# Fourteen of the 64 pieces of w2 split among the experts instead of in the blocks before them, with ScalarE issuing their transfers

## The chip, the core and the metric

The kernel runs on one core of a Trainium2 chip. The metric is the device time of one execution in microseconds (us); lower is better. The profile counts the granted TensorE clock as a share of 2.4 GHz: 1.00 is 2.4 GHz, 0.50 is 1.2 GHz.

## The reference

Three layers follow each other, all in float32 at the outside.

1. Attention without a softmax: for each of 8 batches and 8 heads, `kv = k^T v`, `out = q kv`, and each row of `out` is divided by its root mean square and multiplied by `g_norm`. This gives `x` with 4608 rows (8 x 576 tokens) and 512 columns.
2. A dense layer: `h = x w_in` (2048 columns), `g = h cos(h)`, `x = g w_out` (512 columns).
3. A mixture of 8 experts: for each token the gate `x w_gate` chooses one expert; the expert computes `relu(x w1[e]) w2[e]` (512 to 1024 to 512 columns), and the row is multiplied by the gate's probability.

## The kernel before

Every float32 matrix product is made of float16 products: an operand is split into a high and a low half, and three matmuls (high by high, high by low, low by high) are summed in PSUM. A split is one ScalarE instruction (high half) and, behind it, one VectorE instruction (low half); the helper `split` holds both, at lines 103 and 104.

The work runs in two parts.

**Blocks 0 to 8.** Each block takes 512 of the 4608 tokens through the dense layer, in 32 steps; the code calls a step `hs`, and step h of block b has the number 32 b + h in the lists below. In each step TensorE makes a part of the dense layer's two products for this block, while the other engines prepare the attention of the next block, split its k and v (tiles ks), and route the block before to the experts. The order of everything is written out by hand: lists say in which step a helper is called. From block 4 on the dense layer's first product is made with seven products for eight (tiles sx and sy, results h); it reads sums of weights that `w_fac` (block 2 and 3) and `w_fac4` (block 3 and 4, the fourth sum, four groups g of three steps i) make on VectorE. Block 3 lies at about 315 to 403 us, block 4 up to 487, block 5 up to 572, block 6 up to 656, block 7 up to 745, block 8 up to 827.

**Experts 0 to 7.** For each expert the tokens' rows come from DRAM (`load_x`), then come the first product (`e_g1` for expert 0, `e_g1q` for the others, again seven products for eight, tiles qx and qy), relu, the second product (`e_g2`, and `e_g2t` for the last 96 rows), and the scatter to the result. Meanwhile the weight sums and row sums of the next expert are made (`prepare`, with the lists `prep0`, `prep` and `side`: "f" is a split of a weight sum, "s" a sum, "x" and "y" the row sums). `e_g1q` calls `side` four times, twice for each of two groups.

**w2.** The second weights of all experts are 64 pieces of 128 x 512 float32 (piece i belongs to expert i // 8). Each is loaded by `w2_load` (256 KB), split by `w2_split` into a high and a low half, and stored by `w2_store` to the DRAM array `w2x` (256 KB); `load_w2x(e)` later brings all halves of an expert back. `W2_AT` lists the step of each piece's split; all 64 stand in blocks 2 to 8. The first 51 use the pools w2p (loads, two buffers) and w2q (halves, tile w2o, two buffers), and the load of piece i + 2 is issued behind the split of piece i. The 13 of block 8 use free places of xring in the same manner. A store is issued two steps after its split, in block 8 one step after. All these transfers are issued on SP, in the order of the program, with all other loads, stores and transposes.

At the start of block 7 SP also loads all kv matrices at once (`load_kv_all`, tile kvall, eight transfers of 256 KB). In the blocks 4 and 5 the pieces of k and v are split in the steps of `KV_AT` (five pairs: k, v) and multiplied in those of `KV_MM` (tile kvps).

Of the kernel before, what the change touches and what calls it, by code (L numbers as in the profile page):

```python
# [9 lines left out]
F32 = mybir.dt.float32  # L10
# [26 lines left out]
def tile_attn_moe_moe(ctx: ExitStack, tc: tile.TileContext, q, k, v, g_norm, w_in, w_out, w_gate, w1, w2, out):  # L37
    nc = tc.nc
    B, H, S, D = q.shape
    NT, DM = out.shape  # L40
# [3 lines left out]
    E, _, F2 = w1.shape  # L44
    KD = DM // 128
    NFB = DFF // 128
    NF2 = F2 // 128
# [6 lines left out]
    FAST = 4  # L54
# [17 lines left out]
    w2x = dram.tile([E, 128, 2, 4096], F16, name="w2x")  # L72
# [39 lines left out]
    def now(f):  # L112
        if f is not None:
            f()
# [36 lines left out]
    xring = ctx.enter_context(tc.tile_pool(name="xring", bufs=1)).tile([128, 11 * 1024], F16, name="xring")  # L151
# [8 lines left out]
    pools = {}  # L160
# [812 lines left out]
    w2st, w2o = {}, {}  # L973

    def w2_place(n):

        n = (x_slot(NB - 1, "11") + 7 + n) % 11
        return xring[:, n * 1024:n * 1024 + 1024]

    def w2_load(i):  # L980

        e, fb = divmod(i, NF2)
        if i < W2_LAST:
            w2st[i] = pools["w2p"].tile([128, DM], F32, tag="w2i", name="w2i")
        else:
            w2st[i] = w2_place(i % 2).bitcast(F32)
        nc.sync.dma_start(out=w2st[i], in_=w2[e, fb * 128:(fb + 1) * 128, :])

    def w2_split(i):
        if i < W2_LAST:  # L990
            w2o[i] = pools["w2q"].tile([128, 2, DM], F16, tag="w2o", name="w2o")
        else:
            w2o[i] = w2_place(2 + i % 2).rearrange("p (a c) -> p a c", a=2)
        lo = split(w2o[i][:, 0], w2o[i][:, 1], w2st.pop(i), S_W2)

        def late():
            lo()
            if i + 2 < W2_LAST or W2_LAST <= i < E * NF2 - 2:
                w2_load(i + 2)

        return late

    def w2_store(i):
        e, fb = divmod(i, NF2)
        nc.sync.dma_start(out=w2x[e, :, :, fb * DM:(fb + 1) * DM], in_=w2o.pop(i))

    def load_w2x(e):
        if e < 2:
# [10 lines left out]
    def load_x(e, r0=0, r1=CAP):  # L1019
        if r0 == 0:  # L1020
            xeT[e] = xtp.tile([128, 2 * KD, CAP], F16, name="xeT")
            fld[e] = xsm.tile([128, CT, FLD], F32, name="fld")
        rows = slice(e * NT + r0, e * NT + r1)
        nc.sync.dma_start_transpose(out=xeT[e][:, :, r0:r1], in_=xs.bitcast(F16)[rows, 0:2 * DM])
        i0, i1 = r0 // 128, (r1 + 127) // 128
        nc.sync.dma_start(out=fld[e][:, i0:i1],
                          in_=xs[e * NT + i0 * 128:e * NT + i1 * 128, DM:ROW].rearrange("(i p) c -> p i c", p=128))
# [39 lines left out]
    HC = CAP // 2  # L1067
# [63 lines left out]
    def e_g1q(e, side):  # L1131

        h1[e] = (h1p.tile([128, NF2, CAP], F16, name="h1h"), h1p.tile([128, NF2, CAP], F16, name="h1l"))
        hh, hl = h1[e]

        def out(p, r, src):
            nc.scalar.activation(out=hh[:, p, r], in_=src, func=AF.Relu)
            return lambda: nc.vector.scalar_tensor_tensor(out=hl[:, p, r], in0=src, scalar=0.0, in1=hh[:, p, r],
                                                          op0=ALU.max, op1=ALU.subtract)

        r0, r1, both = slice(0, HC), slice(HC, CAP), slice(0, CAP)
        for g in range(2):
            st = []
            for n in range(2):
                p = 2 * g + n
                x, y = [(psm if n else psh).tile([128, HC], F32, tag="m" if n else "h", name=nm) for nm in ("qx", "qy")]
                e_prod(e, 1, p, x, first=True)
                t5, t1 = [b3.tile([128, HC], F32, tag=tag, name="qt") for tag in "nu"]
                nc.scalar.activation(out=t1, in_=x, func=AF.Copy)
                st.append((p, x, y, t1, t5, wq["hc"][n]))  # L1150
            for p, x, y, t1, t5, hc in st:
                e_prod(e, 2, p, y, first=True)
                nc.vector.tensor_tensor(out=hc[:, 1], in0=y, in1=t1, op=ALU.add)
            side()
            tvs = []
            for p, x, y, t1, t5, hc in st:
                e_prod(e, 6, p, x)
                tvs.append(b2.tile([128, HC], F32, tag="yT", name="qt"))
                nc.scalar.activation(out=tvs[-1], in_=x, func=AF.Copy)
                e_prod(e, 5, p, y, first=True)  # L1160
                nc.scalar.activation(out=t5, in_=y, func=AF.Copy)
            side()
            late = []
            for (p, x, y, t1, t5, hc), tv in zip(st, tvs):
                e_prod(e, 7, p, x)
                e_prod(e, 3, p, y)
                c22 = b3.tile([128, HC], F32, tag="u", name="c22")
                nc.vector.tensor_tensor(out=c22, in0=x, in1=t5, op=ALU.add)
                nc.vector.tensor_tensor(out=hc[:, 0], in0=y, in1=tv, op=ALU.add)
                now(out(p + 4, r0, c22))  # L1170
                late.append(out(p, both, hc[:, 0:2].rearrange("p r c -> p (r c)")))
            late[0]()
            for p, x, y, t1, t5, hc in st:
                e_prod(e, 4, p, x)
                now(out(p + 4, r1, x))
            late[1]()
# [85 lines left out]
    for e in range(E):  # L1262
        for c in range(2):
# [20 lines left out]
    FAC_AT = {h: divmod(i, 6) for i, h in enumerate(  # L1284
        [64 + h for h in (0, 1, 2, 4, 6, 8, 10, 12, 14, 16, 18, 24, 26, 28, 30)] + [
            96 + h for h in (0, 1, 2, 6, 8, 10, 12, 14, 16)])}
    FAC4_AT = [(g, i, 32 * (FAST - 1) + h) for g, hs in enumerate(((20, 21, 21), (24, 25, 25), (32, 41, 42), (43, 47, 48)))
               for i, h in enumerate(hs)]
    W2_AT = [64 + 7 * i // 3 for i in range(14)] + [98 + 7 * i // 2 for i in range(9)] + [32 * n + h for n, hs in (
        (4, (30, 31)), (5, (2, 9, 11, 15, 31)), (6, (2, 9, 10, 15, 17, 19, 25, 27, 30, 31)),  # L1290
        (7, (2, 3, 9, 10, 15, 17, 19, 25, 27, 30, 31)), (8, (3, 6, 9, 10, 13, 15, 17, 19, 22, 23, 25, 27, 30))) for h in hs]
    W2_LAST = sum(h < 256 for h in W2_AT)
    KV_AT = ((16, 17), (17, 18), (19, 19), (26, 27), (27, 30))
    KV_MM = (19, 21, 22, 30)

    with tc.manual_schedule():
        pump()
# [35 lines left out]
        for b in range(NB):  # L1333
# [83 lines left out]
            if b == 1:  # L1417
                todo = [("g", 1, AHEAD), ("y", 0, NFB - 2), ("y", 0, NFB - 1), ("g", 1, AHEAD + 1)]
                ys = [("y", 1, f) for f in range(NFB - LAG)]

                for f in range(AHEAD + 2, NFB):
                    n = 2 if f < AHEAD + LAG + 2 else f - LAG - 2 - ys[0][2] + 1
# [97 lines left out]
            if b >= FAST:  # L1520
# [16 lines left out]
                for hs in range(32):  # L1537
                    g, step = divmod(hs, 8)
# [48 lines left out]
                f()  # L1587
        fac.close()
        p2r = ExitStack()
        h1p = p2r.enter_context(tc.tile_pool(name="h1p", bufs=1, side="right", reuse_waits="tile"))  # L1590
        obp = p2r.enter_context(tc.tile_pool(name="obp", bufs=4, side="right", reuse_waits="tile"))
        wq["hc"] = [xring[:, o:o + 4 * HC].bitcast(F32).rearrange("p (r c) -> p r c", r=2)
# [10 lines left out]
        ranks = [call(r_rank, b)] + [call(r_scatter, b, t) for t in range(4)] + [  # L1603
            call(load_x, e, HEAD, CAP) for e in range(2)] + [call(gates_x, 0, 0, HEAD // 128)]
        hold.append(1)
        prep0 = {4: ("f0",), 5: ("s2",), 6: ("f1",), NF2 + 3: ("x1", "y1", "f6", "f3")}
        prep = (("f1", "x0", "s3", "f4"), ("y0", "x1"), ("f5", "y1", "f2"), ("f6", "f3"), ())
        side = (("s0", "f0"), ("s1",), ("s2",), ())
        later = {}

        def prepare(e, items):
            for it in items:
                if it == "gates":
                    later.pop(it)()
                    continue
                n = int(it[1:])
                if it[0] == "x":
                    later[e, n] = x_sums(e, n)
                elif it[0] == "y":
                    later.pop((e, n))()  # L1620
                else:
                    {"s": w_sums, "f": w_split}[it[0]](e, n)
# [24 lines left out]
        turn, put = e_g2t(0)  # L1647
        turn()
        load_x(2)
        for e in range(1, E):  # L1650
            todo = list(side) if e + 1 < E else []
            if e == 1:
                todo = [(), ("s0",), ("f0", "gates"), ("s1", "s2")]
                later["gates"] = call(gates_x, 1)
                put0 = put
            e_g1q(e, lambda: todo and prepare(e + 1, todo.pop(0)))
            if e + 1 < E:
                load_w2x(e + 1)
            if 2 < e + 2 < E and e + 2 > 2 and e + 2 not in xeT:
                load_x(e + 2)  # L1660
            for n, i in enumerate((0, None, 1, 2, 3)):
                if e + 1 < E:
                    prepare(e + 1, prep[n])
                if i is None:
                    turn, put = e_g2t(e)
                    turn()
                else:
                    e_g2(e, i)
                if n == (3 if e + 1 < E else 2):
                    put()  # L1670
                if e == 1 and n == 3:
                    put0()
            if e + 1 < E:
                gates_x(e + 1)
# [83 lines left out]
```

## Time and profile before

| | |
|---|---|
| three runs | 1222.55, 1223.27, 1223.70 us (median 1223.27) |
| the profiled execution | 1221.86 us, of which the span from the first to the last instruction is 1220.0 |
| busy in the span: TensorE, VectorE, ScalarE, POOL | 1177.7, 906.2, 694.4, 359.0 us |
| mean granted TensorE clock | 0.991 |
| moved by DMA | 188.37 MB, a mean of 154 GB/s |

An engine's busy time is the time in which one of its instructions ran. The end of a matmul is modelled, so rows of matmuls overlap: what separates them is the distance of their starts. Times in the views are counted from the start of the span. A row ends with the idle time of the engine just before it and what ended that idle time, in square brackets or behind the last bar. PE is TensorE, DVE is VectorE, ACT is ScalarE, SP is SyncE; SPq and ACTq are instructions of their queues, such as the issue of a DMA.

### The profile page before, as it was taken

What the parts mean: (1) busy time and instruction counts of PE and PEld (TensorE: products, weight loads), DVE (VectorE), ACT (ScalarE), POOL (GpSimd) and SP (SyncE); (2) the same over time, 40 slices, a digit from 0 to 9 for tenths busy, and PEclk for the clock granted to TensorE, in tenths of its full rate; (3) what the DMA queues carried; (4) which work ended last, traced back from release to release, by engine and by line L of the source; (5) the groups of instructions that cost most, each with busy time, mean ns of one, the idle gap of its engine ahead of it and who ended that gap; (6) DMA issues with size and microseconds to landing.
All of it is one profiled execution on the core that took longest, in us unless ns stands there. A gap on an engine that the chain in (4) does not pass through costs nothing.

```text
span 1220.0 us, 22013 instructions
## 1 busy us (share of the span) xinstructions
PE 1177.7 (97%) x8612; PEld 718.4 (59%) x8612; DVE 906.2 (74%) x1468; ACT 694.4 (57%) x1220; POOL 359.0 (29%) x367
## 2 busy tenths in 40 slices
PE   6989999999999999999998999999999999999996
PEld 6534445444444676666665666665776576576663
DVE  4789955888969798888776676684687777777740
ACT  3665663666666766766755756663455455455441
POOL 1123423334434344244253243251102102102111
PEclk8999999999999999999999999999999999999998
DMA  9669816776754745756538548548396365363001
GB/s 292 209 184 314 263 25 150 203 147 160 196 122 115 181 92 110 178 113 149 130 90 237 167 96 226 139 131 226 85 283 213 78 192 188 71 202 117 27 24 52
DMA packets 278882, 188.37 MB, mean 154 GB/s; under 512 B 209646, under 2 KB 244462, under 8 KB 278768
## 3 DMA queue, kind: packets, MB, share of 16 engines
q1 hardware_dynamic: 272128, 167.68, 53.0%
q0 software_dynamic: 5952, 19.18, 4.4%
q8 instruction: 69, 1.13, 0.4%
q14 instruction: 45, 0.37, 0.1%
q10 hardware_dynamic: 688, 0.02, 0.0%
HBM read 97.86 MB, written 49.38 MB: 121 GB/s over the span
## 4 chain that ended last, share of the span: by engine, by line
PE 76%; DVE 8%; issue 6%; ACT 4%; DMA 3%; POOL 2%; SPq 0%; POOLq 0%; ACTq 0%; DVEq 0%
PE yps L817 12%; PE ops L117 4%; PE ops L119 4%; PE ops L118 4%; PE hps L118 4%; PE hps L119 4%; PE hps L117 4%; PE yps L117 4%; PE yps L119 4%; PE yps L118 4%; PE sx L117 2%; PE sx L118 2%; PE sx L119 2%; PE qx L119 2%; PE qx L117 2%
## 5 line engine op out<-in xcount | busy, mean ns | idle before, releaser
L783 POOL TENSOR_TENSOR gl<-n,gh 128x512 f16<-128x512 f32 x80 | 96.1, 1202 | 248.5 <-ACT gh L782 199.7
L764 POOL TENSOR_TENSOR gl<-u,gh 128x512 f16<-128x512 f32 x64 | 90.2, 1409 | 225.7 <-ACT gh L763 177.8
L1194 POOL DMA_INDIRECT out_dram<-ob,ei x40 | 48.4, 1211 | 302.5 <-ACT ob L1192 281.8
L817 PE MATMUL yps<-woh,gh 128*128 128x512 f16 x328 | 124.8, 380 | 0.5 <-DVE yrow L104 0.4
L817 PE MATMUL yps<-woh,gl 128*128 128x512 f16 x328 | 124.7, 380 | 0.3 <-POOL gl L783 0.3
L817 PE MATMUL yps<-wol,gh 128*128 128x512 f16 x328 | 124.8, 380 | 0.0
L817 PEld LDWEIGHTS <-gh 128*128 128x128 f16 x656 | 63.6, 98 | 64.6 <-issue 2.4
L117 PE MATMUL hps<-xring,wih 128*128 128x512 f16 x256 | 97.0, 379 | 3.3 <-DVE u L766 3.3
L118 PE MATMUL hps<-xring,wih 128*128 128x512 f16 x256 | 97.0, 379 | 1.0 <-ACT xring L577 0.9
L119 PE MATMUL ops<-w2h,h1l 128*128 128x512 f16 x256 | 97.0, 379 | 0.0
L118 PE MATMUL ops<-w2l,h1h 128*128 128x512 f16 x256 | 97.0, 379 | 0.0
L117 PE MATMUL ops<-w2h,h1h 128*128 128x512 f16 x256 | 97.0, 379 | 0.0
L119 PE MATMUL hps<-xring,wil 128*128 128x512 f16 x256 | 97.0, 379 | 0.0
L117 PE MATMUL yps<-woh,gh 128*128 128x512 f16 x248 | 94.0, 379 | 0.2 <-DVE yrow L104 0.2
L119 PE MATMUL yps<-woh,gl 128*128 128x512 f16 x248 | 94.0, 379 | 0.0
L118 PE MATMUL yps<-wol,gh 128*128 128x512 f16 x248 | 94.0, 379 | 0.0
L118 PEld LDWEIGHTS <-wih 128*128 128x128 f16 x576 | 56.5, 98 | 46.9 <-issue 13.0
L778 DVE SCALAR_TENSOR_TENSOR n<-h,n 128x512 f32<-128x512 f32 x60 | 63.9, 1065 | 20.3 <-ACT n L777 18.0
L117 PEld LDWEIGHTS <-wih 128*128 128x128 f16 x576 | 56.5, 98 | 35.5 <-issue 0.7
L119 PEld LDWEIGHTS <-wil 128*128 128x128 f16 x576 | 56.5, 98 | 35.4 <-DVE wst L286 1.2
L782 ACT ACTIVATE gh<-n 128x512 f16<-128x512 f32 x80 | 50.5, 631 | 32.4 <-DVE n L780 32.4
L779 ACT ACTIVATE n<-n,half_pi 128x512 f32<-128x512 f32 x80 | 57.6, 720 | 17.3 <-DVE n L778 17.3
(281 smaller groups left out, 3325.5 us busy)
## 6 DMA issues: line engine op xcount, KB each, us to landing
w1s<-in_moe_w_dram SPq DMA_DIRECT2D x16, 1024.0 KB
w2i<-in_moe_w_dram SPq DMA_DIRECT2D x51, 256.0 KB
w2x<-w2o SPq DMA_DIRECT2D x51, 256.0 KB
xs<-pre SPq DMA_DIRECT2D x8, 1320.0 KB
wst<-in_moe_w_in_dram SPq DMA_DIRECT2D x8, 1024.0 KB
wst<-in_moe_w_out_dram SPq DMA_DIRECT2D x8, 1024.0 KB
w2h<-w2x SPq DMA_DIRECT2D x16, 512.0 KB
w2l<-w2x SPq DMA_DIRECT2D x16, 512.0 KB
```

Of the source, the lines that this page charges most:

```text
L117: nc.tensor.matmul(out=o, lhsT=ah, rhs=bh, start=first, stop=False, **kw)
L118: nc.tensor.matmul(out=o, lhsT=ah, rhs=bl, start=False, stop=False, **kw)
L119: nc.tensor.matmul(out=o, lhsT=al, rhs=bh, start=False, stop=last, **kw)
L764: nc.gpsimd.tensor_tensor(out=gl, in0=u, in1=gh, op=ALU.subtract)
L778: lambda: nc.vector.scalar_tensor_tensor(out=u, in0=h, scalar=sc, in1=n, op0=ALU.mult, op1=ALU.subtract),
L779: lambda: nc.scalar.activation(out=u, in_=u, func=AF.Sin, scale=SIN_SCALE, bias=half_pi),
L782: lambda: nc.scalar.activation(out=gh, in_=u, func=AF.Copy),
L783: lambda: nc.gpsimd.tensor_tensor(out=gl, in0=u, in1=gh, op=ALU.subtract))
L817: nc.tensor.matmul(out=yps[b][t], lhsT=g[k][:, o:o + 128], rhs=w[fb // 8][:, (fb % 8) * 512:(fb % 8) * 512 + 512], start=first and i == 0, ...
L1194: d = nc.gpsimd.indirect_dma_start(out=out, out_offset=bass.IndirectOffsetOnAxis(ap=eid[e, i][r], axis=0), in_=ob[r], in_offset=None, boun ...
```

## The change

- Pieces 50 to 63 of w2 leave `W2_AT`; the other 50 stand there with new steps: 14 in block 2 as before, then 8, 1, 4, 7, 7 and 9 in blocks 3 to 8 (before: 9, 2, 5, 10, 11 and 13).
- The fourteen are loaded into one place of xring, split into a tile w2o of a pool of one buffer (w2r), and stored. Their loads and stores are issued on ScalarE's queue. A new function `piece(e, n)` is called in nine turns n of each expert e from 1 on: it stores the piece that was split before, issues the next load, and in turns 2, 5 and 8 (5 and 8 in expert 1) splits a piece. Turns 0 to 3 are the four calls of `side` in `e_g1q`, turns 4 to 8 stand before the five parts of the second product.
- Groups 0 and 1 of the fourth weight sum move from steps 20, 21, 21 and 24, 25, 25 of block 3 to 17, 18, 20 and 21, 22, 24.
- The third v piece of blocks 4 and 5 is split in step 21 instead of 19, and its matmuls are called in step 23 instead of 22.
- In expert 0 the weight split f1 for expert 1 is made before the second tile of the second product instead of behind the seventh tile of the first.

```diff
         else:
-            w2st[i] = w2_place(i % 2).bitcast(F32)
-        nc.sync.dma_start(out=w2st[i], in_=w2[e, fb * 128:(fb + 1) * 128, :])
+            w2st[i] = (w2_place(i % 2) if i < len(W2_AT) else xring[:, 32 * HC:32 * HC + 1024]).bitcast(F32)
+        queue = nc.sync if i < len(W2_AT) else nc.scalar
+        queue.dma_start(out=w2st[i], in_=w2[e, fb * 128:(fb + 1) * 128, :])
 
     def w2_split(i):
-        if i < W2_LAST:
+        if i < W2_LAST or i >= len(W2_AT):
             w2o[i] = pools["w2q"].tile([128, 2, DM], F16, tag="w2o", name="w2o")
...
-            if i + 2 < W2_LAST or W2_LAST <= i < E * NF2 - 2:
+            if i + 2 < W2_LAST or W2_LAST <= i < len(W2_AT) - 2:
                 w2_load(i + 2)
...
     def w2_store(i):
         e, fb = divmod(i, NF2)
-        nc.sync.dma_start(out=w2x[e, :, :, fb * DM:(fb + 1) * DM], in_=w2o.pop(i))
+        queue = nc.sync if i < len(W2_AT) else nc.scalar
+        queue.dma_start(out=w2x[e, :, :, fb * DM:(fb + 1) * DM], in_=w2o.pop(i))
...
-    FAC4_AT = [(g, i, 32 * (FAST - 1) + h) for g, hs in enumerate(((20, 21, 21), (24, 25, 25), (32, 41, 42), (43, 47, 48)))
+    FAC4_AT = [(g, i, 32 * (FAST - 1) + h) for g, hs in enumerate(((17, 18, 20), (21, 22, 24), (32, 41, 42), (43, 47, 48)))
                for i, h in enumerate(hs)]
-    W2_AT = [64 + 7 * i // 3 for i in range(14)] + [98 + 7 * i // 2 for i in range(9)] + [32 * n + h for n, hs in (
-        (4, (30, 31)), (5, (2, 9, 11, 15, 31)), (6, (2, 9, 10, 15, 17, 19, 25, 27, 30, 31)),
-        (7, (2, 3, 9, 10, 15, 17, 19, 25, 27, 30, 31)), (8, (3, 6, 9, 10, 13, 15, 17, 19, 22, 23, 25, 27, 30))) for h in hs]
+    W2_AT = [64 + 7 * i // 3 for i in range(14)] + [32 * n + h for n, hs in (
+        (3, (4, 7, 9, 11, 13, 15, 29, 31)), (4, (30,)), (5, (9, 11, 15, 31)), (6, (9, 11, 15, 17, 25, 27, 30)),
+        (7, (9, 11, 15, 17, 25, 27, 30)), (8, (3, 6, 9, 11, 13, 17, 22, 23, 27))) for h in hs]
...
-    KV_AT = ((16, 17), (17, 18), (19, 19), (26, 27), (27, 30))
-    KV_MM = (19, 21, 22, 30)
+    KV_AT = ((16, 17), (17, 18), (19, 21), (26, 27), (27, 30))
+    KV_MM = (19, 21, 23, 30)
...
         p2r = ExitStack()
+        pools["w2q"] = p2r.enter_context(tc.tile_pool(name="w2r", bufs=1, side="right", reuse_waits="tile"))
...
-        prep0 = {4: ("f0",), 5: ("s2",), 6: ("f1",), NF2 + 3: ("x1", "y1", "f6", "f3")}
+        prep0 = {4: ("f0",), 5: ("s2",), NF2 + 1: ("f1",), NF2 + 3: ("x1", "y1", "f6", "f3")}
...
         load_x(2)
+        w2_load(len(W2_AT))
+        rest2 = list(range(len(W2_AT), E * NF2))
+
+        def piece(e, n):
+
+            if w2o:
+                w2_store(*w2o)
+                if rest2:
+                    w2_load(rest2[0])
+            if n in ((5, 8) if e == 1 else (2, 5, 8)) and rest2:
+                now(w2_split(rest2.pop(0)))
+
...
-            e_g1q(e, lambda: todo and prepare(e + 1, todo.pop(0)))
+            turns = list(range(9))
+
+            def side_work():
+                piece(e, turns.pop(0))
+                if todo:
+                    prepare(e + 1, todo.pop(0))
+
+            e_g1q(e, side_work)
...
                     prepare(e + 1, prep[n])
+                piece(e, turns.pop(0))
```

## Rows read from the trace of the kernel before

**Rows 1.** Stages (block 3, block 7, experts 1 to 7): length, each engine's busy us.

```profile
core 0: us, PE busy (x) PEld busy (x) DVE busy (x) ACT busy (x) POOL busy (x), PEclk, DMA share, GB/s
315.00:403.00 88.00, 85.29 (x550) 41.29 (x549) 72.47 (x124) 54.98 (x99) 34.90 (x30) 1.00 0.63 150
...
656.00:745.00 89.00, 84.21 (x681) 55.15 (x679) 61.49 (x103) 54.29 (x98) 32.91 (x30) 0.96 0.65 162
...
884.00:1210.00 326.00, 324.56 (x2511) 208.11 (x2509) 230.96 (x378) 158.49 (x274) 47.27 (x73) 1.00 0.46 134
```

**Rows 2.** TensorE's waits, 315 to 830 us: total us, times, longest.

```profile
PE sx L117 <- DVE h L1559: 7.4, 6, 4.4
PE kvps L347 <- DVE ks L104: 2.2, 1, 2.2
...
PE kvps L347 <- ACT ks L103: 0.4, 1, 0.4
PE yps L817 <- POOL gl L783: 0.3, 1, 0.3
```

**Rows 3.** TensorE's waits, 884 to 1210 us.

```profile
PE qx L117 <- DVE c L1168: 0.2, 1, 0.2
```

**Rows 4.** TensorE in order of time: start, length, instruction, idle before.

```profile
460.25 0.27 PE L117 MATMUL sx<-xring,wih 128*128 128x256 f16 x1 [1.09 <-DVE h L1559]
...
544.37 0.27 PE L117 MATMUL sx<-xring,wih 128*128 128x256 f16 x1 [0.57 <-DVE h L1559]
...
627.59 0.27 PE L117 MATMUL sx<-xring,wih 128*128 128x256 f16 x1 [0.43 <-DVE h L1559]
...
666.49 0.38 PE L817 MATMUL yps<-woh,gl 128*128 128x512 f16 x1
671.22 0.37 PE L117 MATMUL sx<-xring,wih 128*128 128x256 f16 x1 [4.35 <-DVE h L1559]
...
717.21 0.27 PE L117 MATMUL sx<-xring,wih 128*128 128x256 f16 x1 [0.44 <-DVE h L1559]
```

**Rows 5.** The 5 us behind the longest wait, columns as in rows 1.

```profile
671.20:676.20 5.00, 4.99 (x18) 2.60 (x18) 3.97 (x7) 4.67 (x9) 0.73 (x1) 0.50 0.47 161
```

**Rows 6.** ScalarE in order of time, 661 to 668 us.

```profile
661.13 0.62 ACT L103 ACTIVATE nat<-qst 128x512 f16<-128x512 f32 x1
667.63 0.63 ACT L103 ACTIVATE w2o<-w2i 128x512 f16<-128x512 f32 x1 [5.89 <-DMA w2x<-w2o]
```

**Rows 7.** SP's queue in order of time, 656 to 662 us.

```profile
656.49 4.62 SPq L230 DMA_DIRECT2D kvall<-kvx  x8
661.16 1.25 SPq L1005 DMA_DIRECT2D w2x<-w2o  x2
```

**Rows 8.** VectorE in order of time, block 3 and block 4.

```profile
390.18 0.68 DVE L104 SCALAR_TENSOR_TENSOR ks<-vst,ks 128x512 f16<-128x512 f32 x1
...
457.84 1.75 DVE L104 SCALAR_TENSOR_TENSOR ks<-vst,ks 128x512 f16<-128x512 f32 x1
459.52 0.68 DVE L1559 TENSOR_TENSOR h<-sx,t 128x512 f32<-128x512 f32 x1
```

**Rows 9.** The chain that ended last, 621 to 625 us: start, length, what.

```profile
621.74 3.09 DMA w2x<-w2o
```

**Rows 10.** Instructions on tile w2o: count, duration in ns (min/median/max).

```profile
L103 ACT ACTIVATE w2o<-w2i x51: 612/616/667, 226.4 to 743.7; 128x512 f16<-128x512 f32 x51
L104 DVE SCALAR_TENSOR_TENSOR w2o<-w2i,w2o x51: 674/685/1649, 227.2 to 745.0; 128x512 f16<-128x512 f32 x51
L1005 SPq DMA_DIRECT2D w2x<-w2o x51: 518/575/1497, 229.7 to 746.7; - x51
```

**Rows 11.** ScalarE and its queue, the first 12 us.

```profile
0.94 0.56 ACTq L1301 DMA_DIRECT2D gs<-in_g_norm_dram  x1
```

**Rows 12.** ScalarE in order of time at an expert's start.

```profile
977.03 0.42 ACT L1149 ACTIVATE qt<-qx 128x304 f32<-128x304 f32 x1
...
990.98 0.42 ACT L1159 ACTIVATE qt<-qx 128x304 f32<-128x304 f32 x1 [1.84 <-PE qx L119]
```

**Rows 13.** Busy time in 5 us at an expert's start, columns as in rows 1.

```profile
975.00:980.00 5.00, 5.00 (x37) 3.47 (x36) 2.21 (x9) 3.21 (x6) 2.07 (x4) 1.00 0.94 381
```

## The prediction

> **What bounds the kernel now.** I read the table by stages first. In blocks 3 to 8 and in experts 1 to 7 TensorE is busy for nearly the whole stretch: 85.3 of 88 us in block 3, 84.2 of 89 in block 7, 324.6 of 326 in the experts, while VectorE and ScalarE have slack everywhere (72.5 and 55.0 of 88 in block 3; 231.0 and 158.5 of 326 in the experts) [rows 1]. The diff touches no matmul, so only TensorE's waits can shrink or grow. The second view is the list of those waits. From 315 to 830 us the ones that matter are: products into sx that wait for VectorE's h (7.4 us, six times, 4.4 the longest), kvps for the ks pieces (2.2 behind VectorE, 0.4 behind ScalarE) and one yps for POOL's gl (0.3) [rows 2]. In the experts there is one, of 0.2 us [rows 3]. So there is something to win in the blocks, and a nearly flawless stretch to spoil in the experts.
>
> Third, TensorE in order of time shows where the waits lie: 1.09 us at 460 (block 4), 0.57 at 544 (block 5), 0.43 at 627 (block 6), 4.35 at 671 and 0.44 at 717 (block 7) [rows 4]. The matmul rows last 0.38 us but follow each other by 0.22 when nothing waits, so a wait costs some 0.16 more than its bracket: from 666.49 to 671.22 are 4.73 us, where 0.22 would do. After that longest wait the granted clock is 0.50, the lower level (1.2 GHz), for the next 5.0 us [rows 5]; 5.0 us at half clock do 2.5 us of work, so 2.5 more are lost. The whole event costs 4.35 + 0.16 + 2.5 = 7.0 us.
>
> Fourth, its cause, one engine at a time. ScalarE ends a nat piece at 661.75 and starts the high half of a w2 piece only at 667.63, after 5.89 us of waiting for a store w2x<-w2o: the ring w2o has two buffers, and the store that frees the next one had not landed [rows 6]. That store was issued on SP at 661.16, after eight kvall loads that took the queue from 656.49 to 661.11 [rows 7]. VectorE then does the low halves late, h after them, and TensorE waits for h.
>
> **The change, part by part.**
>
> *Fewer w2 pieces in the blocks.* In block 6 they stood in steps 30 and 31 and in block 7 in steps 2 and 3: four in a row around the kvall loads. Now the last of block 6 is in step 30 and the next in step 9 of block 7; at 89/32 = 2.8 us a step that is about 681 us, some 13 us after the late store landed. Nothing on ScalarE waits for a w2o buffer near 661 any more: minus 7.0 us. Pieces in step 19 of blocks 6 and 7 also go; steps 20 to 22 are where h is made and needed, and the waits at 627 and 717 are there: 0.43 + 0.44 + 2 x 0.16 = 1.2 us. The end of block 8 loses its pieces of steps 25 and 30, ahead of the gl wait: 0.3 + 0.16 = 0.5 us. If another piece or chain stands in the same place, these are nothing; if all go they are as stated.
>
> *w2 and the fourth weight sum in block 3.* The wait of kvps is for a low half of v that VectorE begins at 390.18 [rows 8]. Ahead of it in the same queue stood two w2 pieces (steps 19 and 23) and both late sums of w_fac4, group 1 (steps 24 and 25). The pieces leave that stretch: at 0.685 us each they give 1.4 us [rows 10]. The sums move to steps 17 to 24, partly onto time in which VectorE idled. Needed are 2.2 + 0.4 + 0.16 = 2.8 us: I take all of it, since the relief is 1.4 us and the sums besides; the lower bound is 1.4.
>
> *The v piece from step 19 to 21, its matmuls from 22 to 23 (blocks 4 and 5).* At 457.84 VectorE does this v half (1.75 us), and h follows at 459.52, with TensorE waiting 1.09 us for it [rows 4, 8]. With the piece behind h, h starts 1.75 us sooner, and the wait goes; in block 5 the same, with 0.57. Together 1.09 + 0.57 + 2 x 0.16 = 2.0 us. The cost is that kvps now needs this v two steps later, and the chain of the next h tile lies behind it; two steps are the distance that the other pieces of these blocks have already.
>
> Sum of the gains: 7.0 + 1.2 + 0.5 + 2.8 + 2.0 = 13.5 us.
>
> *Fourteen pieces in the experts.* Each is 0.616 us on ScalarE and 0.685 on VectorE (its longest row 1.65) [rows 10]. A store's issue holds its queue for 0.52 to 1.50 us, median 0.575 [rows 10]; the three that ScalarE issued itself at the start begin with one of 0.56 [rows 11]. So ScalarE gets 14 x 0.616 + 28 x 0.57 = 24.6 us (with 1.5 an issue, 50.6), VectorE 14 x 0.685 = 9.6 (at most 23). In 326 us ScalarE goes from 158 to 183 (209), VectorE from 231 to 241 (254): neither becomes the bound. What hides a piece is the gap at its place: in the first half of a product group ScalarE waits 1.84 us for TensorE before its next copy [rows 12], which covers a split (0.62) or a store and a load (1.14), not one of 3.0. If that cover is gone the copy of qx is late, and TensorE, which accumulates into the same bank, after it. A landing took 3.09 us when the way was free [rows 9], and load and split lie two turns apart: 326 us / 7 experts / 9 turns = 5.2 us a turn, some 10 us on the mean. Lower bound of the cost 0, upper bound the rival below; I take 0.5 us.
>
> The page "DMA: Bandwidth & Descriptors", section "Issuing engines are not separate DMA queues", of the Trainium skill says that transfers from all issuing engines share the same 16 DMA engines and interleave. By it the move to ScalarE's queue buys no bandwidth, but a piece needn't wait for everything that SP issued earlier; no row of before shows two busy queues side by side. If instead the two w1s and four w2x loads that SP issues at an expert's start (4.2 MB by their tiles) went first at 381 GB/s, the rate at 975 us [rows 13], the load of turn 0 would land about 11 us late, about when turn 2 splits it; by the one the sum is unchanged, by the other a hold of one or two us is possible four times.
>
> *The rest.* One split (f1) moves from the sixth product of expert 0 to before its second output tile: no wait of TensorE stands at its old place, so 0. The wider pool on the right side: 0, since nothing is written there before the blocks' last readers are through. SP issues 28 transfers fewer before 830 us; counted above.
>
> *Given back.* TensorE will come sooner to places where others were just in time. I leave three waits of the small size seen now (0.43, 0.44, 0.57) [rows 4]: 1.5 us with the 0.5 of the experts 2.0. Net: 13.5 - 2.0 = 11.5 us.
>
> The profiled execution took 1221.86 us (span 1220.0, 1.86 around it): 1221.86 - 11.5 = 1210.4. The median of the runs, 1223.27, stands 1.4 above it, so I predict 1211.8.
>
> **The rivals.**
>
> *The event of block 7 stays in another form.* The eight kvall loads are still there, and behind them the qT transposes and whatever waits for them. For it: the queue is as full as before. Against it: only the w2 buffer was waited for. All other gains then hold: 1211.8 + 7.0 = 1218.8.
>
> *Given back altogether.* VectorE is the late engine in nearly all waits [rows 2]; if its pace set these blocks, a wait removed would return some steps later. Against it: 72.5 of 88 and 61.5 of 89 us are no full engine [rows 1]. It would give 1223.3, no change.
>
> *Slower: ScalarE held by its own queue.* Its transfers wait in line with its copies. Place: turn 0 of an expert, where the store of the piece from turn 8 and the next load are issued between qx copies (as the copy at 977.03 [rows 12]), while the DMA engines are 0.94 busy [rows 13]; the split of turn 2 then waits for that load and, with one w2r buffer, for that store. Price: block 7 shows it, a hold of 5.89 us on ScalarE [rows 6] cost 7.0. One such hold leaves 1218.8; it decides from two on: 1211.8 + 14.0 = 1225.8. For it: the experts have no other slack on TensorE, and 28 issues give as many places. Against it: the distance of two turns, some 10 us from turn 0 to 2, against a landing of 3.09.
> The Trainium skill's page "TensorE: Matmul & The Clock Gate", in the section "Architectural detail: the array is 16× 32×32, not 1× 128×128", calls ScalarE a strict FIFO, and the trace agrees (nothing of ScalarE ran in those 5.89 us).
>
> **How the numbers follow.** Forecast 0.62, its own range 1208.5 to 1215: at the low end nothing is given back (1223.3 - 13.5 = 1209.8) and the waits that I left standing go as well; at the high end block 3 gives only 1.4 and two more us return. The event in another form, or one hold in the experts: 0.17, at 1218.8. Given back: 0.08, at 1223.3. Two holds or more: 0.10, at 1225.8 and above; some 0.03 lie elsewhere. A measurement tells about 0.2% (2.4 us) from no change: faster 0.81, same 0.09, slower 0.10. The range of 8 in 10 takes the first two cases: 1208.5 to 1219.5.
>
> **What would show it.** In the profile after: the list of TensorE's waits from 315 to 830 us holds no sx wait of 4 us and no granted clock of 0.5 between 660 and 690; ScalarE has no wait for w2x<-w2o of several us in block 7; kvps waits under 0.5 us; no sx wait near 460 or 544. In the experts the list stays near 0.2 us, and ScalarE shows no wait for a DMA. Wrong would be: a wait of ScalarE for a landing of a w2 piece or store in the experts with qx products late behind it, or a new wait of several us in block 7.

## The result, and the profile after

The changed kernel takes 1211.91 us (median of 6 runs, 1209.85 to 1214.57), the kernel before in the same session 1223.15 (6 runs, 1222.12 to 1224.47): ratio 0.9909, 95% interval 0.9899 to 0.9919, so 11.2 us less. The profiled execution took 1213.22 us, with a span of 1211.3. The two spans differ by 8.7 us only, because the profiled execution of before was 1.3 us under this median and that of after 1.3 over its own: whoever takes the 11.2 us apart by profiles finds 8.7 of them.

The page of the changed kernel first: busy time, share of the span and instructions of each engine, then ScalarE's queue (q10: packets, MB, share of the DMA engines).

```profile
PE 1177.2 (97%) x8612; PEld 718.8 (59%) x8612; DVE 906.9 (75%) x1468; ACT 696.5 (58%) x1220; POOL 359.0 (30%) x367
...
q10 hardware_dynamic: 6512, 7.36, 1.9%
```

No engine has clearly less work than before (TensorE 0.5 us less, VectorE 0.7 and ScalarE 2.1 more); 7.36 MB run on ScalarE's queue. So over the whole span the gain is waiting time of TensorE. Its waits in the changed kernel (us in total, times, longest), from 315 to 830 us and, below the second dots, from 810 to 875 (expert 0):

```profile
PE kvps L347 <- DVE ks L104: 1.5, 2, 1.1
PE hps L117 <- DVE u L766: 0.6, 2, 0.3
PE sx L117 <- DVE h L1561: 0.5, 1, 0.5
...
PE rps L886 <- DVE pc L875: 0.4, 1, 0.4
...
PE h1ps L117 <- DMA xeT<-xs: 1.2, 1, 1.2
PE lps L846 <- DMA ob<-yrow: 1.1, 2, 0.8
```

Against [rows 2] the 7.4 us of sx are 0.5, but the 2.2 + 0.4 of kvps have become 1.5 with two new waits beside them (hps, rps), and expert 0 has a wait for xeT that wasn't there. From 875 us to the end there is none at all.

Block 7, with the columns of [rows 1], shows the same:

```profile
656.00:745.00 89.00, 89.00 (x736) 59.72 (x734) 62.63 (x103) 55.81 (x99) 34.67 (x33) 1.00 0.64 167
```

It is full, at a clock of 1.00 where it was 0.96; block 3 is as it was (TensorE busy for 85.5 of 88 us, before 85.3). Where each stage starts is read from the first matmul of its product: the first of the two times in a row is the start of the first of the group. First the kernel before (blocks 4, 6, 8; experts 0 and 1):

```profile
L117 PE MATMUL sx<-xring,wih x4: 272/272/273, 402.6 to 403.6; 128*128 128x256 f16 x4
L117 PE MATMUL sx<-xring,wih x4: 273/273/273, 570.1 to 571.1; 128*128 128x256 f16 x4
L117 PE MATMUL sx<-xring,wih x4: 272/272/273, 742.0 to 743.0; 128*128 128x256 f16 x4
L117 PE MATMUL h1ps<-xeT,w1h x32: 326/326/326, 824.7 to 845.0; 128*128 128x384 f16 x32
L117 PE MATMUL qx<-xeT,wqh x8: 292/293/293, 882.6 to 894.7; 128*128 128x304 f16 x8
```

and the changed kernel, with the second chunk of expert 0's tokens ahead of expert 1:

```profile
L117 PE MATMUL sx<-xring,wih x4: 272/273/273, 402.9 to 403.8; 128*128 128x256 f16 x4
L117 PE MATMUL sx<-xring,wih x4: 272/272/273, 568.8 to 569.8; 128*128 128x256 f16 x4
L117 PE MATMUL sx<-xring,wih x4: 272/272/273, 732.4 to 733.4; 128*128 128x256 f16 x4
L117 PE MATMUL h1ps<-xeT,w1h x32: 326/326/326, 814.3 to 834.6; 128*128 128x384 f16 x32
L117 PE MATMUL h1ps<-xeT,w1h x32: 257/259/259, 855.4 to 864.3; 128*128 128x224 f16 x32
L117 PE MATMUL qx<-xeT,wqh x8: 292/293/293, 873.8 to 885.9; 128*128 128x304 f16 x8
```

The differences of neighbouring starts, before and after:

| stage | before | after | change | predicted |
|---|---|---|---|---|
| up to block 4 | 402.6 | 402.9 | +0.3 | -2.8 |
| blocks 4 and 5 | 167.5 | 165.9 | -1.6 | -2.0 |
| blocks 6 and 7 | 171.9 | 163.6 | -8.3 | -7.0 - 1.2 |
| block 8 | 82.7 | 81.9 | -0.8 | -0.5 |
| expert 0 | 57.9 | 59.5 | +1.6 | 0 |
| experts 1 to 7, to the end of the span | 337.4 | 337.5 | +0.1 | +0.5 |
| three small waits, anywhere | | | | +1.5 |

Two lines are off: between these two profiles block 3 gave nothing, and expert 0 took 1.6 us back. The stretch ahead of block 3 plays no part: the same hps matmul near 311 us starts at 311.3 before and at 311.4 after.

### The profile page after: what moved, and what is told of

It reads as the page before. It is cut to its first block, busy times and chain, and to the rows that moved or that the text cites. A ratio compares the mean times of both kernels' runs of the same rounds, so it can differ in the third digit from the quotient of the medians.

```text
span 1211.3 us, 22014 instructions
## 1 busy us (share of the span) xinstructions
PE 1177.2 (97%) x8612; PEld 718.8 (59%) x8612; DVE 906.9 (75%) x1468; ACT 696.5 (58%) x1220; POOL 359.0 (30%) x367
## 3 DMA queue, kind: packets, MB, share of 16 engines
q10 hardware_dynamic: 6512, 7.36, 1.9%
## 4 chain that ended last, share of the span: by engine, by line
PE 79%; DVE 6%; issue 5%; ACT 3%; DMA 3%; POOL 2%; SPq 0%; POOLq 0%; DVEq 0%; ACTq 0%
PE yps L817 15%; PE ops L117 4%; PE hps L118 4%; PE ops L119 4%; PE ops L118 4%; PE hps L119 4%; PE hps L117 4%; PE yps L117 3%; PE yps L119 3%; PE yps L118 3%; PE sx L117 3%; PE sx L118 3%; PE sx L119 3%; PE qx L117 2%; PE qx L119 2%
## 5 line engine op out<-in xcount | busy, mean ns | idle before, releaser
L778 DVE SCALAR_TENSOR_TENSOR n<-h,n 128x512 f32<-128x512 f32 x60 | 66.9, 1115 | 20.3 <-ACT n L777 19.2
L779 ACT ACTIVATE n<-n,half_pi 128x512 f32<-128x512 f32 x80 | 57.5, 719 | 19.5 <-DVE n L778 19.5
```

The lines of the kernel that those rows point to most:

```text
L778: lambda: nc.vector.scalar_tensor_tensor(out=u, in0=h, scalar=sc, in1=n, op0=ALU.mult, op1=ALU.subtract),
L779: lambda: nc.scalar.activation(out=u, in_=u, func=AF.Sin, scale=SIN_SCALE, bias=half_pi),
```

## The experiments

Times are medians, each with the ratio to the kernel before run beside it. Unless said otherwise an experiment starts from the changed kernel.

### The same kernel again

> The changed kernel again, so that the undoings have it beside them on the same chip. First profile: span 1211.3 us, 8.7 less than before, while the medians differ by 11.2. My theory (the gain is made of waits of TensorE in blocks 4 to 8 and nothing in block 3) expects about 1212, 10 to 12 under before, with the first product of block 4 at 403 us as in both profiles. The rival, that block 3 does give 2.8 us and the one profile hid it, expects the first product of block 4 near 400.

1212.69 us, ratio 0.9911 (0.9892 to 0.9930). Block 4 starts at 403.1, so the profile of the changed kernel hid nothing. That the one profile of the kernel before may be the unusual one, this expectation did not allow for; the next experiment comes to it.

### Block 3: the sums back, the pieces gone

```diff
-    enumerate(((17, 18, 20), (21, 22, 24), (32, 41, 42), (43, 47, 48)))
+    enumerate(((20, 21, 21), (24, 25, 25), (32, 41, 42), (43, 47, 48)))
```

> The changed kernel with the fourth weight sum's groups 0 and 1 back in steps 20, 21, 21 and 24, 25, 25 of block 3; the w2 pieces stay as changed. My prediction's step (pieces and sums together give 2.8 us in block 3) expects it slower by 1 to 2 us, with the kvps wait back to over 1 us in one place. The rival, which the first profile suggests: VectorE has the same work before the same matmuls, and the earlier sums only make two hps waits (0.3 each), one of rps (0.4) and leave 1.5 of kvps; then the undoing costs nothing, 0 plus or minus 0.7 us, with one kvps wait of 1 to 2 us in place of the five small ones.

1213.4 us, ratio 0.9917 (0.9897 to 0.9937): not told from the changed kernel by its time. TensorE's waits in its block 3:

```profile
PE kvps L347 <- DVE ks L104: 2.5, 2, 2.2
PE kvps L347 <- ACT ks L103: 0.5, 1, 0.5
```

and the window behind them (columns as in [rows 1]), with a granted clock of 0.66:

```profile
392.00:397.00 5.00, 5.00 (x24) 1.98 (x21) 3.20 (x6) 2.81 (x5) 2.47 (x4) 0.66 0.41 108
```

With the sums back and the w2 pieces still gone, the 2.2 us of kvps stand as before. So taking the pieces out of that stretch gives nothing by itself, where I had 1.4 us as the lower bound. What holds this v half is the sums. In this kernel's order of time (VectorE, then ScalarE):

```profile
379.44 0.69 DVE L632 TENSOR_TENSOR x<-xsum,x 128x512 f32<-128x512 f32 x1 [1.16 <-POOL x L632]
...
390.92 0.68 DVE L104 SCALAR_TENSOR_TENSOR ks<-vst,ks 128x512 f16<-128x512 f32 x1
...
387.56 0.63 ACT L103 ACTIVATE wih<-ft 128x512 f16<-128x512 f32 x1 [1.02 <-DVE ft L720]
...
388.62 0.61 ACT L103 ACTIVATE ks<-vst 128x512 f16<-128x512 f32 x1
```

VectorE works nearly without a pause from 379.44 to the low half of v at 390.92, and four instructions of the late sum (0.69, 1.65, 0.68 and 0.69 us) stand in that stretch. They make the wait of 2.2 us: the changed kernel differs from this one in the steps of the sums alone, and has no such wait. On ScalarE the high half of the sum waits for VectorE, and the high half of v stands behind it in the queue: the 0.5 us. In the kernel before the stretch ran from 378.10 to 390.18. The piece that left it (step 23) made it 0.6 us shorter, but measured from the hps matmul near 311 us it now begins 0.9 us later, behind the wait for POOL; why, no run parts (the pieces left in block 3 have new steps as well). The other piece that I had counted (step 19, on VectorE at 367.23) stood ahead of that pause and so was never in the stretch.

Moving the sums cures that, but in the changed kernel they are now ahead of the next links (VectorE, then the waits of TensorE):

```profile
374.14 1.75 DVE L718 TENSOR_TENSOR ft<-wih,wfh 128x512 f32<-128x512 f16 x1
...
377.03 0.68 DVE L766 SCALAR_TENSOR_TENSOR u<-hps,u 128x512 f32<-128x512 f32 x1
...
377.77 0.38 PE L117 MATMUL hps<-xring,wih 128*128 128x512 f16 x1 [0.29 <-DVE u L766]
384.94 0.60 PE L347 MATMUL kvps<-ks 128*128 128x64 f16 x15 [1.11 <-DVE ks L104]
```

u comes late, and with it pc (a wait of rps, 0.4 us) and the v half before: the wait has moved 6 us ahead and been split, not removed.

The split still matters for the clock. Four kernels with a profile have the sums in their old steps: the one before, this one, and the two of "Only the event" below. All four have nearly the same waits there (0.3 to 0.5 and 2.2 us). The window behind them in the kernel before and in those two (for this one it stands above):

```profile
392.00:397.00 5.00, 5.00 (x39) 2.52 (x38) 4.95 (x9) 4.42 (x9) 2.11 (x3) 1.00 0.59 159
...
392.00:397.00 5.00, 5.00 (x18) 1.95 (x17) 3.54 (x7) 3.12 (x7) 2.28 (x3) 0.72 0.55 159
...
392.00:397.00 5.00, 4.37 (x26) 1.85 (x26) 4.78 (x8) 3.16 (x6) 1.88 (x2) 0.68 0.52 143
```

| profiles | from the hps matmul near 311 us to the first sx matmul of block 4 | clock, 392 to 397 us |
|---|---|---|
| old steps, kernel before | 91.3 us | 1.00 |
| old steps, the three others | 93.0, 93.0, 93.4 us | 0.72, 0.68, 0.66 |
| new steps, all ten | 90.9 to 91.8 us | 1.00 |

The profile of before, on which the stage table rests, is the only one of the four in which the clock did not fall. Against the other three the moved sums are worth some 2 us of block 3. How often the clock falls there in executions without a profile is not shown; the medians of this run and of the changed kernel beside it (1213.4 and 1212.69) lie 0.7 us apart, which is not clear of noise.

### The v piece back

```diff
-    KV_AT = ((16, 17), (17, 18), (19, 21), (26, 27), (27, 30))
-    KV_MM = (19, 21, 23, 30)
+    KV_AT = ((16, 17), (17, 18), (19, 19), (26, 27), (27, 30))
+    KV_MM = (19, 21, 22, 30)
```

> The changed kernel with the third v piece of blocks 4 and 5 back in step 19 and its matmuls in step 22. My prediction's step expects it slower by 2.0 us, with waits of sx for h of about 1.1 us near 460 and 0.6 near 544. The rival, that the fewer w2 pieces already took those waits away (block 5 lost one, block 4 one), expects no wait there and no difference.

1214.1 us, ratio 0.9920 (0.9901 to 0.9939). The interval doesn't part it from the changed kernel, the profile does. In blocks 4 and 5 TensorE waits three times for h, where the changed kernel has one wait of 0.5:

```profile
PE sx L117 <- DVE h L1561: 2.2, 3, 1.1
```

Two of the three are those of [rows 4], 1.09 us at 460 and 0.57 at 544; the third, 0.5 near 416 us, stands in the changed kernel and in the one before as well. Blocks 4 and 5 take 167.5 us again. The term of 2.0 is 1.7 by these rows and 1.6 by the stage table.

### The four pieces around the kvall loads back

```diff
-        (6, (9, 11, 15, 17, 25, 27, 30)), (7, (9, 11, 15, 17, 25, 27, 30))
+        (6, (9, 11, 15, 17, 25, 30, 31)), (7, (2, 3, 15, 17, 25, 27, 30))
```

> The changed kernel with the number of w2 pieces in blocks 6 and 7 as changed, but two of each put back around the kvall loads: steps 30, 31 of block 6 and 2, 3 of block 7 (27, 9 and 11 left out for them). My theory, that the place of the pieces beside the kvall loads makes the event of block 7, expects it slower by 7.0 us, with a ScalarE wait for w2x<-w2o of 5 to 6 us, an sx wait of some 4 us and a granted clock of 0.5 behind it. The rival, that the smaller number of pieces in these blocks (7 and 7 for 10 and 11) gave the gain, expects under 1 us.

1216.31 us, ratio 0.9937 (0.9914 to 0.9960). ScalarE's and TensorE's waits in block 7:

```profile
ACT w2o L103 <- DMA w2x<-w2o: 4.5, 1, 4.5
...
PE sx L117 <- DVE h L1561: 3.0, 1, 3.0
```

and the window in which the wait ends:

```profile
666.00:671.00 5.00, 3.40 (x16) 2.04 (x16) 4.66 (x7) 3.08 (x6) 1.00 (x2) 0.73 0.67 210
```

The event is back link by link: the store, ScalarE, h, TensorE, the lower clock. It is smaller: 3.0 us of wait, not 4.35; blocks 6 and 7 take 168.4 us where the changed kernel takes 163.6; and the medians of the two, run beside each other, are 3.6 us apart. The pieces around these four stayed thinner than before; that this is the reason is not shown. The number of pieces in these blocks is that of the changed kernel, so the rival that the number alone gave the gain is out.

### Only the event: two places for three pieces, from the kernel before

```diff
-        (6, (2, 9, 10, 15, 17, 19, 25, 27, 30, 31)), (7, (2, 3, 9, 10, 15, 17, 19, 25, 27, 30, 31))
+        (6, (2, 9, 10, 13, 15, 17, 19, 25, 27, 30)), (7, (9, 10, 12, 13, 15, 17, 19, 25, 27, 30, 31))
```

> The kernel before with one part alone: the pieces of step 31 of block 6 and of steps 2 and 3 of block 7 moved to step 13 of block 6 and 12 and 13 of block 7; all 64 stay in the blocks, all on SP. My theory expects 5 to 7 us less than before (the event of block 7 goes, the denser steps 9 to 13 may cost some of it). The rival, that ScalarE's wait moves with the pieces because SP stays as full, expects under 2 us.

1236.88 us, ratio 1.0110 (1.0091 to 1.0129): slower than before, and my theory fell in this form. Waits of blocks 6 and 7:

```profile
ACT w2o L103 <- DMA w2x<-w2o: 19.1, 3, 6.5
...
PE sx L117 <- ACT tv L1553: 5.6, 2, 2.8
```

Packed into steps 9 to 19, the pieces wait for their stores there. So the second try puts the same three into block 4, which has two:

```diff
-        (4, (30, 31)),
+        (4, (3, 6, 24, 30, 31)),
-        (6, (2, 9, 10, 15, 17, 19, 25, 27, 30, 31)), (7, (2, 3, 9, 10, 15, 17, 19, 25, 27, 30, 31))
+        (6, (2, 9, 10, 15, 17, 19, 25, 27, 30)), (7, (9, 10, 15, 17, 19, 25, 27, 30, 31))
```

> The kernel before with three w2 pieces less around the kvall loads: step 31 of block 6 and steps 2 and 3 of block 7 go, steps 3, 6 and 24 of block 4 come; all 64 pieces stay in the blocks. Own theory (the event of block 7 is the crowd of pieces at the kvall loads, and a ring of two buffers holds only where pieces are dense; block 4 has room): the 5.9 us wait of ScalarE for w2x<-w2o and the 4.4 us sx wait in block 7 are gone, 5 to 7 us less than before, 1216 to 1218. Rival (w2 pieces are too many for blocks 6 and 7 however they are placed, and taking three away moves the hold to the next dense place): a hold of over 4 us elsewhere in block 7, within 2 us of before.

1217.07 us against 1224.03 of before beside it, ratio 0.9938 (0.9921 to 0.9954): 7.0 us less, the size of the event. Blocks 6 and 7 take 164.8 us where they took 171.9. In block 7 ScalarE waits once for a store, and TensorE once, for 0.4 us:

```profile
ACT w2o L103 <- DMA w2x<-w2o: 2.2, 1, 2.2
```

All 64 pieces are still in the blocks: what costs is not their number but how many stand in a row with SP's eight loads in between, while two buffers take turns.

### The fourteen on SP's queue

```diff
-        queue = nc.sync if i < len(W2_AT) else nc.scalar
+        queue = nc.sync
```

> The changed kernel with the fourteen pieces' loads and stores issued on SP instead of ScalarE; everything else as changed. Theory: the queue matters because SP waits in line there (for transposes that wait on TensorE or VectorE, up to tens of us in the profile of before), so loads and stores land late, ScalarE holds at the splits for several us, and TensorE loses 3 to 15 us in the experts. Rival: the distance of two turns covers SP's waits as well, and the queue is without effect: 0 plus or minus 1 us.

1248.64 us, ratio 1.0201 (1.0183 to 1.0220): 36.7 us more than the changed kernel, more than either theory had. ScalarE is held at four splits, 31.9 us in all. One of four holds in order of time, on ScalarE and TensorE, and the issues of SP before it:

```profile
929.80 0.63 ACT L103 ACTIVATE w2o<-xring 128x512 f16<-128x512 f32 x1 [7.82 <-DMA xring<-in_moe_w_dram]
...
931.50 0.41 PE L117 MATMUL qx<-xring,wqh 128*128 128x304 f16 x1 [7.54 <-ACT qt L1151]
...
918.87 1.50 SPq L953 DMA_DIRECT2D w1s<-in_moe_w_dram  x2
...
921.33 0.65 SPq L988 DMA_DIRECT2D xring<-in_moe_w_dram  x1
```

and the window behind it, with a clock of 0.57:

```profile
931.00:936.00 5.00, 4.50 (x21) 2.75 (x21) 4.86 (x12) 2.71 (x8) 1.06 (x2) 0.57 0.49 157
```

The load leaves SP at 921.33, behind two w1s loads of 1 MB each, and lands 8.5 us later; the split of turn 8 waits for it, with the first copies of the next expert (qt) in the queue behind. In the changed kernel the load for the same split left 7.5 us earlier, ahead of the w1s loads (ScalarE's queue, then SP's):

```profile
913.84 0.62 ACTq L988 DMA_DIRECT2D xring<-in_moe_w_dram  x1
...
918.64 1.50 SPq L953 DMA_DIRECT2D w1s<-in_moe_w_dram  x2
```

The section "Issuing engines are not separate DMA queues" of the Trainium skill's page "DMA: Bandwidth & Descriptors" says that a second issuing engine saves no more than the time of issuing. Here the measurement differs and decides: the bytes and the DMA engines are the same, and the queue is worth 36.7 us, since an issue on SP stands behind whatever SP is waiting for.

### Only the loads, or only the stores, on SP

One of the two lines above takes `nc.sync`, the other stays.

> The changed kernel with the fourteen loads issued on SP and the fourteen stores still on ScalarE. With both on SP ScalarE waited four times for a landing at the splits of turn 8, 36 us in all. Theory (the load behind SP's stalled queue is what those splits wait for): the same four waits, 1235 to 1250. Rival (the stores, which wait in SP's queue and keep the one w2r buffer, are what holds): within 4 us of the changed kernel.

> The changed kernel with the fourteen stores issued on SP and the fourteen loads still on ScalarE. Theory (the load is what the splits wait for): within 4 us of the changed kernel, SP's queue waiting at the stores for the splits without anyone behind in need, unless a store that stands behind the stalled queue keeps the buffer of w2r; 1211 to 1216. Rival (stores in SP's order hold what stands behind them, or the one buffer): 1235 to 1250.

Loads on SP: 1245.09 us, ratio 1.0175 (1.0157 to 1.0193). Stores on SP: 1246.64 us, ratio 1.0193 (1.0173 to 1.0212). Each alone costs nearly what both do; for the stores my theory was wrong. (The 36 us in the first of these expectations should be 31.9.) ScalarE's waits in the experts with the stores on SP:

```profile
ACT w2o L103 <- DMA w2x<-w2o: 30.4, 4, 7.8
```

The four splits are the same, but what is late is the store, and the one buffer of w2r with it. With the loads on SP the same four waits, 29.3 us, are for the load.

### The loads late

```diff
         load_x(2)
-        w2_load(len(W2_AT))
...
                 w2_store(*w2o)
-                if rest2:
-                    w2_load(rest2[0])
...
+                w2_load(rest2[0])
                 now(w2_split(rest2.pop(0)))
```

> The changed kernel with each load of the fourteen pieces issued right before its split instead of two turns ahead, so that ScalarE is held for a whole landing at each of fourteen places. It prices the slower rival of the prediction. If a hold of ScalarE in the experts costs as much as it did in block 7 (5.89 us of hold, 7.0 us), landings of 3 to 4 us at fourteen places cost 40 to 60 us. My theory now: the experts' products wait for ScalarE only where a copy of qx or a relu comes next, so only the splits of turn 2 (four) and of turn 8 (five) can cost, 1 to 3 us each: 5 to 20 us in all.

1254.77 us, ratio 1.0252 (1.0236 to 1.0268): 42.9 us more. ScalarE and TensorE in the experts:

```profile
ACT w2o L103 <- DMA xring<-in_moe_w_dram: 46.6, 14, 6.8
...
PE qx L117 <- ACT qt L1151: 32.0, 5, 7.8
```

ScalarE is held fourteen times, TensorE five times: only the splits of turn 8, which stand ahead of the next expert's first copies, are paid for. Four of these five are also the longest holds (6.5 to 6.8 us); the nine that cost nothing lasted 1.4 to 2.4 us. The fifth, of 3.3 us, cost TensorE 3.4 us of waiting, so the place counts; whether a hold of 6 us in another turn would be free, no run shows.

### The weight split f1 back, and later

```diff
-        prep0 = {4: ("f0",), 5: ("s2",), NF2 + 1: ("f1",), ...
+        prep0 = {4: ("f0",), 5: ("s2",), 6: ("f1",), ...
```

> The changed kernel with the weight split f1 of expert 1 back behind the seventh product of expert 0. In the changed kernel the last row scatter (xs) of POOL lasts 1.71 us beside VectorE's low half of f1 and the transposes of xeT begin 3.5 us behind its start; before it was 0.98 and 2.8. Theory (f1's new place lengthens the scatter and with it the wait of h1ps for xeT, 1.2 us): the scatter is 0.98 again, the wait some 0.7 us shorter, 0.5 to 0.8 us less than the changed kernel, about 1211.3 where that is 1212. Rival (the wait is the distance from the end of block 8, which no longer has slack, and f1 has nothing to do with it): within 0.3 us of the changed kernel, the wait still above 1 us.

1210.04 us, ratio 0.9885 (0.9868 to 0.9903), the lowest of all; the interval overlaps that of the changed kernel a little, so the profile has to tell. The changed kernel's POOL, VectorE and SP around the last row scatter of expert 0's routing:

```profile
845.88 1.71 POOL L934 DMA_INDIRECT xs<-yrow,di  x1 [0.28 <-POOL yrow L929]
...
845.50 1.23 DVE L104 SCALAR_TENSOR_TENSOR wql<-w1s,wqh 128x1024 f16<-128x1024 f32 x1 [4.16 <-ACT wqh L103]
...
849.37 1.59 SPq L1026 DMA_TRANSPOSE xeT<-xs  x1
```

and the same view with f1 in its old place:

```profile
844.68 0.98 POOL L934 DMA_INDIRECT xs<-yrow,di  x1 [0.28 <-POOL yrow L929]
...
847.44 1.59 SPq L1026 DMA_TRANSPOSE xeT<-xs  x1
```

There expert 0's two chunks start at:

```profile
L117 PE MATMUL h1ps<-xeT,w1h x32: 326/326/326, 813.8 to 834.1; 128*128 128x384 f16 x32
L117 PE MATMUL h1ps<-xeT,w1h x32: 259/259/259, 852.8 to 861.8; 128*128 128x224 f16 x32
```

The scatter is 0.73 us shorter, the transposes follow 2.8 us behind its start instead of 3.5, the wait for xeT is gone, and the second chunk starts 39.0 us behind the first instead of 41.1. Some 0.5 of those 2.1 us are the wait of lps for its rows (0.6, not 1.1), which varies from run to run with f1 in the same place. All of expert 0 takes 57.5 us, the changed kernel's 59.5.

One tile later instead of earlier (`NF2 + 2`):

> The changed kernel with the weight split f1 one output tile of expert 0 later still (before the third tile of the second product, where the changed kernel has it before the second). In every kernel so far with f1 before the second tile the fourth row scatter lasted 1.72 us and h1ps waited 0.6 to 1.4 us for xeT; in every one with f1 in the first product it lasted 0.98 and nothing waited. Theory (what costs is that VectorE's low half of f1 runs beside that scatter, not that f1 left the first product): the scatter is 0.98 again, no wait for xeT over 0.4 us, the time that of the kernel with f1 in its old place, 1209 to 1211.5. Rival (it is the old place that gives the gain, by work in the first product): the wait of about 1 us stays and the time is that of the changed kernel, 1212 to 1213. A third case: the four splits now behind each other ahead of the second chunk hold ScalarE's copies and a new wait of 1 us or more stands at the second chunk's first product.

1212.01 us, ratio 0.9918 (0.9902 to 0.9934). Its scatter lasts 0.98 us. Its wait at the second chunk:

```profile
PE h1ps L117 <- DVE h1l L1067: 0.8, 1, 0.8
```

So the scatter is short and nothing waits for xeT, as the theory had it; the time is not, because the third case came too: VectorE now reaches the second chunk with four splits on its hands and h1l is late; expert 0 takes 58.9 us. A wait of 0.9 us in block 5 for transposed rows came on top, and no run settles where it is from.

## Why the prediction was right, and where it was wrong

*The event of block 7, 7.0 us.* Right in cause and size. Blocks 6 and 7 became 8.3 us shorter, where the event and the two waits of step 19 made 8.2, and the kernel before with only three pieces moved away gained 7.0. The rival that the event stays in another form is out: ScalarE has no wait for w2x<-w2o in block 7 any more.

*Block 3, 2.8 us, lower bound 1.4: the term that failed.* Against the profile of before it came out as -0.3, against the three other profiles with the sums in their old steps as some 2 us, and in neither case by what I had added up. I counted the instructions that leave the stretch and took their time for the wait's. Without the two pieces the wait is 2.2 us still, and the sums, one to three steps ahead now, are late work in front of other readers: 0.6, 0.4, 1.1 and 0.4 us in place of 0.4 and 2.2. What the sums do give is the clock: behind the split wait it fell in none of ten profiles, behind the whole one in three of four. The prediction had no term for that.

*The v piece, 2.0 us.* 1.6 to 1.7: the two waits went (1.09 and 0.57), and the 0.16 for each that I had put on top does not show. *The end of block 8, 0.5:* 0.8.

*Fourteen pieces in the experts, 0.5 us; slower rival from two holds on.* Right in result: +0.1 us, no wait of TensorE behind 875 us. But it is nearer to the rival than I thought: ScalarE waits three times for a load there (2.6 us in all, 1.5 the longest), TensorE not once. The rival's place was wrong. I put it at turn 0 with the split of turn 2 behind; the runs show turn 8, and there a hold costs some 9 us (36.7 / 4 with the transfers on SP, 42.9 / 5 with late loads): 7 of wait and the lower clock behind it. A microsecond of hold costs what it did in block 7 (36.7 for 31.9 us, against 7.0 for 5.89); too small was the hold, for the load issued there landed after 8.5 us (921.33 to 929.80) and not after the 3.09 that I set against two turns. What keeps the change clear of it is that loads and stores leave early on ScalarE's own queue.

*f1, "no wait of TensorE stands at its old place, so 0": wrong.* I looked at the place it leaves and not at the one it goes to. It costs the 1.2 us of the xeT wait and what belongs to it, most of the 1.6 us that expert 0 takes back. In all nine profiles with f1 before the second tile the last scatter is the long one and h1ps waits 0.6 to 1.4 us for xeT; in the four with f1 in its old place neither is there.

*The sum.* 10.7 us of gains by the profiles instead of 13.5, and 2.0 given back, as allowed for, but in two places only. By profiles the net is 8.7 for 11.5, and the whole difference is block 3; the medians say 11.2. That the forecast of 1211.8 fell on the median of 1211.91 is owed in part to the 2.6 us between the profiled executions and their medians, and so to luck. A part of the 2.6 may be the clock of block 3. The profiled execution of before had a mean granted clock of 0.991, and of the 44 executions of that kernel beside the experiments 40 had 0.990 or less. That it was lost in block 3 is not shown.

## What to carry over

An instruction's time is a gain only on the chain that ends last: ask which queue the late reader stood behind, and take that out alone before counting. Two profiles are two executions: behind the same wait the clock fell in three of four, so look at more than one profile of a kernel before you call a term nothing. A step that moves has a cost at its new place, on the neighbours of every engine that it uses. And for a transfer in a full kernel the question is not only what it moves but which queue it stands in, and what that queue is waiting for when the issue's turn comes.

## What the runs showed of the hardware

- An indirect scatter on POOL lasted 1.71 us where VectorE's low half of f1 (1.23 us, two inputs in SBUF) ran since 0.38 us before it, and 0.98 us alone. The section "Who interferes with whom" of the Trainium skill's page "SBUF — State Buffer" says that a VectorE instruction with two SBUF inputs contends with a GpSimd instruction that reads SBUF; the trace agrees: VectorE ended at 846.73, and the scatter 0.86 later, at 847.59.
- Nearly the same wait in block 3 was followed by the lower clock in three profiles and not in a fourth: 0.3 to 0.5 and 2.2 us of waiting, then a granted clock of 0.66, 0.72 and 0.68 from 392 to 397 us, but 1.00 in the kernel before. The profile with 0.66 (the sums put back) had idled 0.3 us more at 383 us; the two with 0.72 and 0.68 have the waits of before and nothing more, so that is not what decides. What does is open.
